# V loads moved to ScalarE's DMA queue, and two more groups of x transposed by DMA

## The chip, the cores and the metric

The kernel runs on one core of a Trainium2 chip. The metric is device time in microseconds (us): a kernel is run several times beside runs of the kernel before on the same chip, and the median is given. All profiles show one execution. The engines are TensorE (PE; its weight loads are PEld), VectorE (DVE), ScalarE (ACT), GpSimd (POOL) and SyncE (SP). DMAs are issued by SyncE, ScalarE or GpSimd; the queue of an issuing engine is written with a q (SPq, ACTq, POOLq).

## The reference, cut to what matters

```python
q, k, v : (8, 8, 576, 64) fp32        # batch, heads, sequence, head_dim
# attention inside chunks of 64 positions
scores = scale * matmul(q_c, k_c.T);  attn = softmax(scores);  out = matmul(attn, v_c)
x = out.transpose(0, 2, 1, 3).reshape(4608, 512)
# FFN with squared ReLU: w_in (512, 2048), w_out (2048, 512)
h = maximum(x @ w_in, 0);  return (h * h) @ w_out
```

## The kernel before

The 4608 tokens are cut into 18 groups of 256. Two groups make a block, which is the unit of the FFN; block 0 holds groups 0 and 1, block 1 groups 3 and 2, block 2 groups 4 and 5, and so on to block 8. While TensorE computes the FFN of block j, the attention of block j+1 is slipped in at fixed "slots" between the FFN's matmul groups, and q, k and v of block j+2 ("far") are loaded.

Each group passes through these steps. The short names are those of the plan of slots.

- Loads of q, k (L110) and v (L117 and L124), from SyncE.
- C: GpSimd casts q and k to bf16 (L217). TD: a DMA transpose turns them (L224, from SyncE).
- SC: scores (L238) on TensorE. AV: values (L259), then the division on VectorE (L269), which gives x.
- XT: x is transposed, either by TensorE with a VectorE copy (L292, L296) or by a DMA from SyncE (L282).

```python
    def transpose_x(g):                                    # XT
        ...
        if g >= FIRST_DMA_X:                               # 6
            for t in range(2):
                x = state.pop(("x", g, t))
                nc.sync.dma_start_transpose(
                    out=xTs[j][:, :, c + t * 128:c + (t + 1) * 128],
                    in_=x.rearrange("p h a d -> p (h a d)"))
            return
        ...                                                # 8 TensorE transposes, 1 VectorE copy
```

ScalarE computes the Relu between the two FFN products, copies the second product out of PSUM and issues the store. All of this is one stream of instructions, in order:

```python
    # ffn_in: first product (L319), Relu (L325), square on VectorE (L326)
            nc.scalar.activation(out=rl[:, 0:n], in_=h[:, 0:n], func=AF.Relu)
    # ffn_out: second product (L335), one token tile of 128 after the other
                    nc.scalar.copy(out=o_sb, in_=o_ps)                      # L352
                    nc.scalar.dma_start(out=out[t0:t0 + 128, :], in_=o_sb)  # L353
```

The block loop takes one load at each slot in `go_slots`, then runs the attention steps planned for that slot. In the built program the DMAs of SyncE and ScalarE draw their completion semaphores from one set of eight, in rotation, and each DMA waits until the one eight places before it has landed, whichever queue issued that one.

The softmax here doesn't subtract the row's maximum and nothing guards it: scores larger than these inputs give would overflow.

Of the kernel before, what the change touches and what calls it, by code (L numbers as in the profile page):

```python
# [17 lines left out]
def kernel(  # L18
# [9 lines left out]
    nc = tc.nc  # L28
# [11 lines left out]

    blocks = [[0, 1], [3, 2]] + [[g, g + 1] for g in range(4, n_grp, 2)]
    FIRST_DMA_T = 4
    FIRST_DMA_X = 6
    BT = GT * max(len(b) for b in blocks)

    const_pool = ctx.enter_context(tc.tile_pool(name="const", bufs=1))
# [28 lines left out]
    def segments(g0, n):  # L75
        while n:
            b, s = divmod(g0, S)
            m = min(n, S - s)
            yield b, s, m
            g0 += m  # L80
            n -= m
# [3 lines left out]
    def runs(g):  # L85

        for t in range(GT // 128):
            p = 0
            for b, s, m in segments(g * GT + t * 128, 128):
                yield t, p, m, b, s  # L90
                p += m

    def qk_pieces(g):
        q_sb = in_pool.tile([128, 2, H, D], FP32, name="q_sb")
        k_sb = in_pool.tile([128, 2, H, D], FP32, name="k_sb")
        qk[g] = (q_sb, k_sb)
        if g < FIRST_DMA_T:

            p = 0
            for b, s, m in segments(g * GT, GT):  # L100
                for dst, src in ((q_sb, q), (k_sb, k)):
                    yield lambda dst=dst, src=src, b=b, s=s, p=p, m=m: nc.sync.dma_start(
                        out=dst.rearrange("p t h d -> p (t h d)")[p:p + m // 2, :].rearrange(
                            "p (h e) -> p h e", h=H),
                        in_=src[b, :, s:s + m, :].rearrange("h (s i) d -> s h (i d)", i=2))
                p += m // 2
            return
        for t, p, m, b, s in runs(g):
            for dst, src in ((q_sb, q), (k_sb, k)):
                yield lambda dst=dst, src=src, b=b, s=s, t=t, p=p, m=m: nc.sync.dma_start(  # L110
                    out=dst[p:p + m, t, :, :],
                    in_=src[b, :, s:s + m, :].rearrange("h s d -> s h d"))

    def v_pieces(g):

        for t, p, m, b, s in runs(g):
            yield lambda t=t, p=p, m=m, b=b, s=s: nc.sync.dma_start(  # L117
                out=v_even[g % NV][p:p + m, t, :, 0:D],
                in_=v[b, 0::2, s:s + m, :].rearrange("h s d -> s h d"))
        for n in {0: [0, 1, 2], 2: [5], 3: [6, 7, 8]}.get(g, [2 * g + 1, 2 * g + 2]):  # L120
            lo, hi = max(0, 128 * n - 64), min(n_tokens, 128 * n + 64)
            p = lo - (128 * n - 64)
            for b, s, m in segments(lo, hi - lo):
                yield lambda n=n, p=p, m=m, b=b, s=s: nc.sync.dma_start(  # L124
                    out=v_odd[n % NO][p:p + m, :, 0:D],
                    in_=v[b, 1::2, s:s + m, :].rearrange("h s d -> s h d"))
                p += m

    def go(pieces):
        for f in pieces:  # L130
            f()
# [143 lines left out]
    def transpose_x(g):  # L275
        j, c = place[g]
        if j not in xTs:
            xTs[j] = att_pool.tile([128, n_dt, BT], BF16, name="xT", bufs=2)
        if g >= FIRST_DMA_X:
            for t in range(2):  # L280
# [20 lines left out]
    SC, AV, XT = scores, values, transpose_x  # L301
# [10 lines left out]
    def ffn_in(j, c, n):  # L312
        if j not in gTs:
            gTs[j] = ffn_pool.tile([128, n_ft, BT], BF16, name="gT")
        gT, xT = gTs[j], xTs[j]
        for ft in range(n_ft):
            h = ps_ffn.tile([128, 512], FP32, name="ps_ffn")
            for dt in range(n_dt):
                nc.tensor.matmul(  # L319
                    out=h[:, 0:n],  # L320
                    lhsT=w_in_bf[:, dt, ft * 128:(ft + 1) * 128],
                    rhs=xT[:, dt, c:c + n],
                    start=(dt == 0), stop=(dt == n_dt - 1))
            rl = ffn_pool.tile([128, 512], BF16, name="rl", bufs=3)
            nc.scalar.activation(out=rl[:, 0:n], in_=h[:, 0:n], func=AF.Relu)  # L325
            nc.vector.tensor_tensor(  # L326
                out=gT[:, ft, c:c + n], in0=rl[:, 0:n], in1=rl[:, 0:n], op=ALU.mult)
            yield

    def ffn_out(j):  # L330
        gT = gTs.pop(j)
        for tt in range(len(blocks[j]) * GT // 128):
            o_ps = ps_ffn.tile([128, d_model], FP32, name="ps_ffn")
            for ft in range(n_ft):
                nc.tensor.matmul(  # L335
                    out=o_ps,
                    lhsT=gT[:, ft, tt * 128:(tt + 1) * 128],
                    rhs=w_out_bf[:, ft, :],
                    start=(ft == 0), stop=(ft == n_ft - 1))
                if ft == n_ft - 1:  # L340
                    t0 = blocks[j][tt // 2] * GT + tt % 2 * 128
                    if j == len(blocks) - 1 and tt == 2 * len(blocks[j]) - 1:
                        for copy, dma, c in ((nc.scalar.copy, nc.scalar, 0),
                                             (nc.vector.tensor_copy, nc.sync, 256)):
                            o_sb = ffn_pool.tile([128, d_model], FP32, name="o_sb", bufs=4)
                            copy(out=o_sb[:, 0:256], in_=o_ps[:, c:c + 256])
                            dma.dma_start(
                                out=out[t0:t0 + 128, c:c + 256], in_=o_sb[:, 0:256])
                        yield
                        continue  # L350
                    o_sb = ffn_pool.tile([128, d_model], FP32, name="o_sb", bufs=4)
                    nc.scalar.copy(out=o_sb, in_=o_ps)  # L352
                    nc.scalar.dma_start(out=out[t0:t0 + 128, :], in_=o_sb)  # L353
                if ft % 4 == 3:
                    yield
# [27 lines left out]
    def pieces(grps):  # L383
        for g in grps:
            yield from qk_pieces(g)
        for g in grps:
            yield from v_pieces(g)
# [27 lines left out]
    for j, grps in enumerate(blocks):  # L415
        nxt = blocks[j + 1] if j + 1 < len(blocks) else []
        far = blocks[j + 2] if j + 2 < len(blocks) else []
        plan = {}

        def at(slot, f, g):  # L420
            plan.setdefault(slot, []).append((f, g))

        if j == 0:
            loads, go_slots = iter(()), []
            for slot, f in ((24, T), (27, SC), (29, AV), (31, XT)):
                at(slot, f, nxt[0])
            at(31, T, nxt[1])
            phases = [ffn_in(0, 0, 512), ffn_out_by_ft(0)]
        elif j == 1:
            go_slots = [*range(17), *range(34, 48)]  # L430
            loads = itertools.chain(pieces(nxt), pieces(far))
            for slot, f in ((2, SC), (6, AV), (11, XT)):
                at(slot, f, grps[1])
            for i, g in enumerate(nxt):
                for slot, f in ((22 + 4 * i, C), (27 + 4 * i, TD), (36, SC), (38 + 2 * i, AV),
                                (42 + 2 * i, XT)):
                    at(slot, f, g)
            phases = [ffn_in(1, 0, 256), ffn_in(1, 256, 256), ffn_out(1)]
        else:
            loads, go_slots = pieces(far), range(32)  # L440
            d = {2: 5, 3: 2}.get(j, 0)
            if j == 2:
                go_slots = [*range(10), *range(18, 32)]
            for i, g in enumerate(nxt):
                for slot, f in ((4, SC), (8, AV), (11, XT)):
                    at(slot + d if f is SC else slot + d + 3 * i, f, g)
            for i, g in enumerate(far):
                at(14 + 2 * i, C, g)
                at(19 + 3 * i, TD, g)
            phases = [ffn_in(j, 0, len(grps) * GT), ffn_out(j)]  # L450
        slot = 0
        for phase in phases:
            for _ in phase:
                if slot in go_slots:
                    for f in loads:
                        f()
                        break
                for f, g in plan.get(slot, []):
                    f(g)
                slot += 1  # L460
        go(loads)
        if j == 1:
            for g in far:
                C(g)
                TD(g)
# [30 lines left out]
```

## Time and profile before

| | before |
|---|---|
| median of the first runs | 303.29 us (300.78 to 303.96, 3 runs) |
| span of the profiled run | 302.7 us |
| TensorE busy | 280.5 us, 93% |
| blocks 2 to 7, start to start | 31.07, 30.50, 30.15, 31.22, 29.36, 29.36 us |
| idle before block 2's first FFN product | none |

Last, from the table by stretch (stretch, its length, busy us and count of each engine, granted clock, DMA share, GB/s), blocks 3 and 5, as the yardstick for later:

```profile
120.65:151.15 30.50, 29.34 (x253) 13.62 (x257) 10.10 (x24) 13.76 (x22) 4.50 (x4) 1.00 1.04 206
...
181.30:212.52 31.22, 29.44 (x254) 13.57 (x257) 11.69 (x24) 12.98 (x22) 4.58 (x4) 1.00 0.93 199
```

TensorE is busy for all but 1.2 us of block 3 and all but 1.8 us of block 5, at full clock.

### The profile page before, as it was taken

The numbers are of one execution on the slowest core, as the hardware profiler recorded it, in microseconds if no ns is written. First come the engines' busy times: TensorE is split into PE (matmuls) and PEld (weight loads), VectorE is DVE, ScalarE is ACT, GpSimd is POOL, SyncE is SP. The second block draws the span as 40 slices with busy tenths as digits, with TensorE's granted clock in tenths as the row PEclk, the third lists the DMA queues.
The fourth block names the chain that finished last, engine by engine and source line by source line (L and its number), as shares of the span: only waits on it lengthen the run. The fifth ranks groups of instructions, "written<-read, shape, count | busy, mean of one in ns | idle before, by whom it ended". The sixth has DMA issues, their size and how long they took to land.

```text
span 302.7 us, 6379 instructions
## 1 busy us (share of the span) xinstructions
PE 280.5 (93%) x2564; PEld 141.3 (47%) x2598; DVE 113.0 (37%) x247; ACT 130.0 (43%) x225; POOL 49.4 (16%) x68
## 2 busy tenths in 40 slices
PE   2889979898899799899999997999999999999995
PEld 2654435784454444444444443444444444444442
DVE  1348613692234350353037203740482038104400
ACT  1536305674217621762176215731662186217511
POOL 2047820140130040023003201400230000000000
PEclk9999999999799999999999999999999999999999
DMA  7999999999999899999899899869997704211011
GB/s 207 243 347 365 342 264 246 237 206 212 217 213 211 194 191 205 224 215 193 195 250 211 148 229 269 171 104 254 267 183 157 182 37 37 69 69 38 0 69 69
DMA packets 158765, 57.04 MB, mean 188 GB/s; under 512 B 139664, under 2 KB 152208, under 8 KB 158736
## 3 DMA queue, kind: packets, MB, share of 16 engines
q1 hardware_dynamic: 153024, 46.81, 73.2%
q10 hardware_dynamic: 5712, 9.83, 10.4%
q8 instruction: 20, 0.33, 0.5%
q14 instruction: 9, 0.07, 0.1%
HBM read 36.70 MB, written 9.44 MB: 152 GB/s over the span
## 4 chain that ended last, share of the span: by engine, by line
PE 67%; DMA 18%; SPq 10%; issue 2%; POOL 1%; ACT 1%; DVE 0%; ACTq 0%
PE ps_ffn L319 31%; PE ps_ffn L335 27%; DMA qkT<-qkb 6%; DMA k_sb<-in_k_dram 6%; SPq L224 4%; DMA w_st<-in_moe_w_in_dram 4%; SPq L282 3%; PE ps_att L259 2%; PE ps_ffn L364 2%; DMA w_st<-in_moe_w_out_dram 2%; PE ps_att L238 2%; SPq L117 1%; PE ps_ffn L164 1%; SPq L124 1%; POOL w_in_bf L139 1%
## 5 line engine op out<-in xcount | busy, mean ns | idle before, releaser
L319 PE MATMUL ps_ffn<-xT,w_in_bf 128*128 128x512 bf16 (+1 forms) x620 | 128.6, 357 | 3.1 <-ACT rl L325 1.6
L326 DVE TENSOR_TENSOR gT<-rl 128x512 bf16<-128x512 bf16 (+1 forms) x160 | 75.5, 489 | 133.9 <-ACT rl L325 131.4
L335 PE MATMUL ps_ffn<-w_out_bf,gT 128*128 128x512 bf16 x500 | 113.0, 382 | 0.8 <-issue 0.3
L325 ACT ACTIVATE rl<-ps_ffn 128x512 bf16<-128x512 f32 (+1 forms) x160 | 86.2, 560 | 42.5 <-PE ps_ffn L319 31.0
L319 PEld LDWEIGHTS <-w_in_bf 128*128 128x128 bf16 x640 | 60.8, 98 | 60.9 <-issue 2.1
L335 PEld LDWEIGHTS <-gT 128*128 128x128 bf16 x512 | 49.9, 98 | 59.7 <-issue 1.3
L352 ACT COPY o_sb<-ps_ffn 128x512 f32<-128x512 f32 x31 | 18.2, 586 | 92.9 <-PE ps_ffn L335 79.7
L217 POOL CAST qkb<-q_sb 128x1024 bf16<-128x1024 f32 x14 | 14.7, 1048 | 146.9 <-DMA q_sb<-in_q_dram 126.6
L269 DVE TENSOR_TENSOR x<-ps_att,rec 128x512 bf16<-128x512 f32 x36 | 24.9, 691 | 1.2
L245 ACT ACTIVATE e<-ps_att 128x1024 bf16<-128x1024 f32 x18 | 18.2, 1037 | 5.5 <-PE ps_att L238 5.5
L217 POOL CAST qkb<-k_sb 128x1024 bf16<-128x1024 f32 x14 | 16.0, 1144 | 6.5 <-DMA k_sb<-in_k_dram 6.4
L364 PE MATMUL ps_ffn<-w_out_bf,gT 128*128 128x512 bf16 x62 | 14.4, 379 | 0.2 <-issue 0.2
L238 PE MATMUL ps_att<-qkT 64*64 64x64 bf16 x576 | 8.1, 198 | 6.0 <-DMA qkT<-qkb 4.6
L266 DVE RECIPROCAL rec<-ps_att 128x8 f32<-128x8 f32 x36 | 7.1, 199 | 15.4 <-PE ps_att L259 15.4
L139 POOL CAST w_in_bf<-w_st 128x1024 bf16<-128x1024 f32 (+1 forms) x9 | 8.8, 980 | 19.1 <-DMA w_st<-in_moe_w_in_dram 19.1
L238 PEld LDWEIGHTS <-qkT 64*64 64x64 bf16 x576 | 6.2, 110 | 10.8 <-DMA qkT<-qkb 6.1
L259 PEld LDWEIGHTS <-e 64*64 64x64 bf16 x576 | 6.8, 110 | 8.5 <-DVE x L269 3.0
L259 PE MATMUL ps_att<-vo_sb,e 64*64 64x65 bf16 x288 | 9.2, 199 | 0.8 <-DMA vo_sb<-in_v_dram 0.8
L364 PEld LDWEIGHTS <-gT 128*128 128x128 bf16 x64 | 6.0, 98 | 7.2 <-issue 0.3
L147 POOL CAST w_out_bf<-w_st 128x1024 bf16<-128x1024 f32 x8 | 8.7, 1091 | 2.7 <-DMA w_st<-in_moe_w_out_dram 2.6
L259 PE MATMUL ps_att<-ve_sb,e 64*64 64x65 bf16 x288 | 9.2, 199 | 0.0
L173 ACT COPY qkT<-ps_att 128x512 bf16<-128x512 bf16 x4 | 2.1, 589 | 13.9 <-DVE qkT L173 11.8
(31 smaller groups left out, 46.0 us busy)
## 6 DMA issues: line engine op xcount, KB each, us to landing
out_dram<-o_sb ACTq DMA_DIRECT2D x35, 256.0 KB, 3.3
q_sb<-in_q_dram SPq DMA_DIRECT2D x25, 256.0 KB, 4.8
k_sb<-in_k_dram SPq DMA_DIRECT2D x25, 256.0 KB, 5.3
ve_sb<-in_v_dram SPq DMA_DIRECT2D x32, 128.0 KB, 3.9
vo_sb<-in_v_dram SPq DMA_DIRECT2D x32, 128.0 KB, 3.9
w_st<-in_moe_w_out_dram SPq DMA_DIRECT2D x8, 512.0 KB, 5.7
w_st<-in_moe_w_in_dram SPq DMA_DIRECT2D x7, 512.0 KB, 7.3
q_sb<-in_q_dram SPq DMA_DIRECT2D x3, 512.0 KB, 6.6
```

The costliest lines, as they stand in the source:

```text
L217: nc.gpsimd.tensor_copy(out=qkb[:, which], in_=qk[g][which].rearrange("p t h d -> p (t h d)"))
L224: nc.sync.dma_start_transpose(out=qkT.rearrange("c w t h q -> c (w t h) q"), in_=qkb.rearrange("p w c -> p (w c)"))
L238: nc.tensor.matmul(out=ps[64 * c:64 * c + 64, o0:o0 + 64], lhsT=qkT[64 * a:64 * a + 64, 1, t, hp, cols], rhs=qkT[64 * a:64 * a + 64, 0, t, ...
L245: nc.scalar.activation(out=e.rearrange("p a h t q -> p (a h t q)"), in_=ps, func=AF.Exp, scale=scale)
L259: nc.tensor.matmul(out=ps[64 * p:64 * p + 64, a, hp * (D + 1):(hp + 1) * (D + 1)], lhsT=e[64 * c:64 * c + 64, a, hp, t, :], rhs=vb[64 * c: ...
L269: nc.vector.tensor_tensor(out=x.rearrange("p h a d -> p a h d"), in0=o[:, :, :, 0:D], in1=rec.to_broadcast([128, 2, n_hp, D]), op=ALU.mult)
L319: nc.tensor.matmul(out=h[:, 0:n], lhsT=w_in_bf[:, dt, ft * 128:(ft + 1) * 128], rhs=xT[:, dt, c:c + n], start=(dt == 0), stop=(dt == n_dt ...
L325: nc.scalar.activation(out=rl[:, 0:n], in_=h[:, 0:n], func=AF.Relu)
L326: nc.vector.tensor_tensor(out=gT[:, ft, c:c + n], in0=rl[:, 0:n], in1=rl[:, 0:n], op=ALU.mult)
L335: nc.tensor.matmul(out=o_ps, lhsT=gT[:, ft, tt * 128:(tt + 1) * 128], rhs=w_out_bf[:, ft, :], start=(ft == 0), stop=(ft == n_ft - 1))
L352: nc.scalar.copy(out=o_sb, in_=o_ps)
L364: nc.tensor.matmul(out=o_ps[tt], lhsT=gT[:, ft, tt * 128:(tt + 1) * 128], rhs=w_out_bf[:, ft, :], start=(ft == 0), stop=(ft == n_ft - 1))
```

## The change

It is meant to relieve two engines. V loads leave SyncE's queue, so that the q/k transposes there are issued earlier. Groups 4 and 5 have their x transposed by DMA as the later groups have, which frees TensorE of 16 transposes. (The change was described as touching groups 2 to 5; the limit that the code moves touches 4 and 5 alone.) The far block's V loads are issued by ScalarE during the second product, one at each slot in `v_slots`.

```diff
-    FIRST_DMA_X = 6
+    FIRST_DMA_X = 4
 ...
-    def v_pieces(g):
+    def v_pieces(g, eng=nc.sync):
 ...   # both V loads: nc.sync.dma_start -> eng.dma_start
         elif j == 1:
-            go_slots = [*range(17), *range(34, 48)]
-            loads = itertools.chain(pieces(nxt), pieces(far))
+            go_slots, v_slots = [*range(17), *range(34, 48)], range(34, 48)
+            loads = itertools.chain(pieces(nxt), *map(qk_pieces, far))
 ...
-                                (42 + 2 * i, XT)):
+                                (41 + 2 * i, XT)):
 ...
         else:
-            loads, go_slots = pieces(far), range(32)
-            d = {2: 5, 3: 2}.get(j, 0)
-            if j == 2:
-                go_slots = [*range(10), *range(18, 32)]
+            go_slots, v_slots = range(16), range(17, 32)
+            loads = itertools.chain(*map(qk_pieces, far))
+            d = {2: 5, 3: 2}.get(j, 1)
 ...
+        v_loads = itertools.chain(*(v_pieces(g, nc.scalar) for g in far if j))
 ...   # at each slot, one of `loads` and one of `v_loads`
         go(loads)
+        go(v_loads)
```

More of the change, by code (lines that the diff above doesn't have):

```diff
@@ L112, in qk_pieces @@
                     in_=src[b, :, s:s + m, :].rearrange("h s d -> s h d"))
-    def v_pieces(g):
+    def v_pieces(g, eng=nc.sync):
         for t, p, m, b, s in runs(g):
-            yield lambda t=t, p=p, m=m, b=b, s=s: nc.sync.dma_start(
+            yield lambda t=t, p=p, m=m, b=b, s=s: eng.dma_start(
                 out=v_even[g % NV][p:p + m, t, :, 0:D],
@@ L123, in v_pieces @@
             for b, s, m in segments(lo, hi - lo):
-                yield lambda n=n, p=p, m=m, b=b, s=s: nc.sync.dma_start(
+                yield lambda n=n, p=p, m=m, b=b, s=s: eng.dma_start(
                     out=v_odd[n % NO][p:p + m, :, 0:D],
@@ L423 @@
         if j == 0:
-            loads, go_slots = iter(()), []
+            loads, go_slots, v_slots = iter(()), [], []
             for slot, f in ((24, T), (27, SC), (29, AV), (31, XT)):
@@ L453 @@
             for _ in phase:
-                if slot in go_slots:
-                    for f in loads:
-                        f()
-                        break
+                for queue, slots in ((loads, go_slots), (v_loads, v_slots)):
+                    if slot in slots:
+                        for f in queue:
+                            f()
+                            break
                 for f, g in plan.get(slot, []):
```

## The prediction

> **What bounds the kernel now.** I began with the page of the kernel before, its busy table and its slices.
>
> ```profile
> PE 280.5 (93%) x2564; PEld 141.3 (47%) x2598; DVE 113.0 (37%) x247; ACT 130.0 (43%) x225; POOL 49.4 (16%) x68
> ...
> PE   2889979898899799899999997999999999999995
> ...
> PEclk9999999999799999999999999999999999999999
> DMA  7999999999999899999899899869997704211011
> ```
>
> TensorE is busy for 93% of the span, and the DMA engines are nearly full until slice 31 of 40. So only TensorE's gaps can be won, together with the one slice in which its clock was at 0.7. Next I read TensorE's timeline, where the gaps stand in brackets.
>
> ```profile
> 76.25 0.45 PE L238 MATMUL ps_att<-qkT 64*64 64x64 bf16 x32 [1.67 <-DMA qkT<-qkb]
> 76.86 2.88 PE L335 MATMUL ps_ffn<-w_out_bf,gT 128*128 128x512 bf16 x7 [0.16 <-issue]
> ...
> 84.36 0.61 PE L292 MATMUL ps_att<-ident,x 128*128 128x128 bf16 x8
> 84.81 1.89 PE L335 MATMUL ps_ffn<-w_out_bf,gT 128*128 128x512 bf16 x8
> 86.54 0.61 PE L292 MATMUL ps_att<-ident,x 128*128 128x128 bf16 x8
> ...
> 100.27 0.45 PE L238 MATMUL ps_att<-qkT 64*64 64x64 bf16 x32 [1.39 <-DMA qkT<-qkb]
> ...
> 128.18 0.45 PE L238 MATMUL ps_att<-qkT 64*64 64x64 bf16 x32 [0.95 <-DMA qkT<-qkb]
> ```
>
> The scores of the second group of a block wait for a DMA transpose of q and k. Blocks 2 to 8 start their first FFN product at 89.58, 120.65, 151.15, 181.30, 212.52, 241.88 and 271.24 us, so blocks 2 to 5 take 31.07, 30.50, 30.15 and 31.22 us. Blocks 6 and 7 take 29.36 each and have no such gap. Against 29.36, blocks 2 to 5 lose 1.71 + 1.14 + 0.79 + 1.86 = 5.5 us in all. That is the most that relief of the queues can give there. Block 5's loss is of another kind: ScalarE's Relu was held for 2.00 us by a k load, because an output store ahead of it in ScalarE's queue waited for that load.
>
> Then I read SyncE's queue, to see why the q/k transposes come late.
>
> ```profile
> 107.74 1.45 SPq L117 DMA_DIRECT2D ve_sb<-in_v_dram  x2
> 109.31 3.92 SPq L282 DMA_TRANSPOSE xT<-x  x2
> 113.29 1.25 SPq L124 DMA_DIRECT2D vo_sb<-in_v_dram  x2
> 114.64 2.57 SPq L282 DMA_TRANSPOSE xT<-x  x2
> 117.31 2.89 SPq L224 DMA_TRANSPOSE qkT<-qkb  x1
> 120.25 0.60 SPq L124 DMA_DIRECT2D vo_sb<-in_v_dram  x1
> 120.95 1.10 SPq L117 DMA_DIRECT2D ve_sb<-in_v_dram  x2
> 122.15 3.62 SPq L224 DMA_TRANSPOSE qkT<-qkb  x1
> ```
>
> V loads stand between the transposes, and the queue is occupied without a break. The transpose begun at 122.15 lands 5.99 us later by the chain, just ahead of the matmul at 128.18.
>
> **What the Trainium skill says.** "DMA: Bandwidth & Descriptors", section "Issuing engines are not separate DMA queues": DMAs of all issuing engines share the same 16 DMA engines, so a second issuer saves only the sequencer's issue time. The trace agrees as far as it goes: a V load takes about 0.6 us of SyncE's queue, and the DMA row is at 8 to 9 tenths however little data moves. "TensorE: Matmul & The Clock Gate", section "Why this matters for your kernels": idle gaps of more than about 3 us drop the clock to half. Here a smaller gap was enough: after the 1.67 us gap seven matmuls took 2.88 us, 0.41 each, against 1.89 us for eight, 0.24 each, at 84.81. The same page, "Architectural detail", calls ScalarE's queue strict FIFO. The held Relu in block 5 agrees, and it matters for every load put on that queue.
>
> **The change, part by part.**
> (1) Transposes of x. The words say groups 2 to 5, but the limit moves from 6 to 4 and the built program loses exactly 16 transpose matmuls (groups 4 and 5) and two VectorE copies. TensorE gets 2 x 0.45 us back by the chain's steps at 84.53 and 86.70, so -0.9 us. The copies (2 x 0.69) were beside other work. Four DMA transposes of 1.2 us issue each, 3.1 us from issue to landing, come on SyncE.
> (2) V loads of the blocks two ahead leave SyncE's queue: 9 to 10 a block, about 0.6 us each, 5 to 6 us. So q/k transposes come earlier, and the waits at 100.27 (1.39), 128.18 (0.95), 156.60 (0.60) and block 5's hold should go, unless something replaces them.
> (3) Eight completion semaphores serve all DMAs of both queues in turn: in the built program each DMA waits for the one eight places before it, on whichever queue. SyncE therefore waits for V loads that ScalarE issues, and the reverse. This decides the seam from block 1 to block 2, where the new x transposes have least time.
>
> The seam, on the clock of the kernel before; the two are alike up to the q/k transposes at 69.10. The second output copy of block 1 runs at 81.47 to 82.06. Behind it ScalarE issues a store (0.4) and then a V load at 82.5. The first x transpose waits for that load by its semaphore; V lands 3.9 us after issue by the page (I take 3.5, as it is alone on its ring), so 86.0. x itself is ready at 81.1, and is not what holds it. After that SyncE's order is fixed: two x transposes (2 x 1.2), a q and a k load (2 x 0.65), two x transposes. The fourth starts at 86.0 + 2.4 + 1.3 + 1.2 = 91.0 (rounded up) and lands 3.1 later, at 94.1. TensorE would be ready for block 2 at 89.58 - 0.9 = 88.7, and its first matmul reads all 512 columns. That is a new stall of 5.4 us, with 4 to 7 within the spread of the landings. The clock should drop after it: the slow stretch after 76.25 cost 7 x 0.19 us plus some 0.5 on what followed, about 1.9 us; I take 1.7.
>
> Block 2 then reaches its scores about 14 us after the last x transpose's issue; q/k transposes for groups 6 and 7 have landed by about 100.5 by the same counting, so the 1.39 goes. At the seam to block 3, the V loads on ScalarE wait for the q/k transposes and a q load on SyncE, and hold the last two output copies: by the same steps the copy of the third token tile ends 16.4 us after block 2's second product starts, when the third FFN group of block 3 wants its bank at 16.0, and the first Relu follows at 17.8. A stall of about 0.6 us takes most of the place of the 0.95. From block 4 on SyncE has some 15 us of issue (8 loads at 0.65, 4 x 1.2, 2 x 2.4) in 29.4, and I find no new wait.
>
> Sum in us: -0.9 (matmuls) +5.4 (stall) +1.7 (clock) -1.4 (block 2) -0.3 (block 3) -0.8 (block 4) -1.9 (block 5) = +1.8. On the median of 303.29 this is 305.1; I shade it to 304.8, because V alone on its ring may land sooner than I took.
>
> **Rivals.** First, the pure gain: x transposes land in time, and the change gives 0.9 + 5.5 = 6.4 us at best, 296.9. For it: SyncE is relieved, and the order of slots has visibly been tuned (x one slot earlier). Against it: after x of group 5 is ready at 84.4 there are under 5 us to the seam, and four x transposes with two loads need 6.1 us of issue plus a landing, even from 84.4. A milder form, a stall of 2 us without clock loss, gives 303.29 - 0.9 + 2 - 4.4 = 300.0. Second, nothing gained on DMA: the 16 engines are the limit (DMA row at 9 tenths), so q/k land no sooner although issued earlier, and waits of 1.39, 0.95 and 0.60 stay beside the new stall: 303.29 - 0.9 + 5.4 + 1.7 = 309.5. Against it: the DMA row falls to 1 to 4 tenths in 0.75 us slices near 103 and 112 us, just where SyncE sits on a wait, so the engines have room. Third, ScalarE becomes the hold: V loads that wait for SyncE's DMAs delay copies and Relu in every block, 1 us for each of six blocks, 311. Against it: the third and fourth copy have some 3 us until their banks are wanted, and V is all issued by mid-product in the later blocks.
>
> **Range and chances.** The stall (4 to 7) and the clock (0 to 2.5) give about 2.5 us each way; block 3's and 4's seams add 1.5, and the runs of before themselves span 3.2. Hence 300.3 to 309.0. Faster by 2% needs 297.2, nearly the whole pure gain: 0.06. Slower by 2% needs 309.4, the second rival or the third: 0.09. The rest is 0.85.
>
> **What would show it.** TensorE's gap before the first FFN product of block 2, released by the x transpose, should be 4 to 7 us, with a PEclk digit below 9 in that slice. SyncE's first x transpose should stand waiting for a V load near 86. The waits of 1.39, 0.95 and 0.60 and the Relu's 2.00 should be absent, and blocks 4 and 5 should be at 29.4 to 29.6. I am wrong if that gap is under 2 us (V lands in 2 us, or the wait is not the one eight back), if blocks 3 to 5 keep waits on q/k, or if Relu or the output copies wait for DMAs in most blocks.

## More of the kernel before

The prediction shows the busy table, the slices, TensorE's timeline and SyncE's queue; they are not repeated. Four other views matter later. First the DMA issues of the kernel before, with count, size, and the median us from issue to landing:

```profile
vo_sb<-in_v_dram SPq DMA_DIRECT2D x32, 128.0 KB, 3.9
...
qkT<-qkb SPq DMA_TRANSPOSE x14, 4.9
```

Next TensorE's entry into block 2. The columns are start, us, engine, line, operation, tiles and count; a bracket at the end would show idle time and its cause. There is none, so block 2 follows block 1 at once:

```profile
89.58 8.80 PE L319 MATMUL ps_ffn<-xT,w_in_bf 128*128 128x512 bf16 x39
```

Third, from the list of waits (us in total, times, longest), the one wait of TensorE on SyncE's DMAs that recurs through the kernel:

```profile
PE ps_att L238 <- DMA qkT<-qkb: 4.6, 4, 1.7
```

## The result and the profile after

| | before | after |
|---|---|---|
| median | 302.12 us (300.78 to 303.96, 4 runs) | 322.79 us (321.31 to 324.49, 4 runs) |
| ratio of fast runs, 95% interval | | 1.0682 (1.0587 to 1.0777) |
| span of the profiled run | 302.7 us | 322.7 us |
| blocks 2 to 7, start to start | 31.07, 30.50, 30.15, 31.22, 29.36, 29.36 | 31.63, 33.78, 32.27, 35.62, 31.89, 29.37 |
| start of block 2 | 89.58 us | 96.82 us |

Ratios here and below are the mean time of one kernel's fast runs over the mean of the other's fast runs of the same rounds, so they are not quite the ratio of the quoted medians. The change is 20 us slower, well outside the predicted range of 300.3 to 309.0.

The page of the kernel after, TensorE, its clock and the DMA engines in 40 slices of 8.1 us:

```profile
PE   2789998998809999599989996999979999999995
...
PEclk9989999999957999999999998799999999999999
DMA  8999999999999779975996699569994960420011
```

The slice at 0 is new, and so are most of the dips that follow it: 5 (from 129 us), 8 (from 161), 6 (from 194) and 7 (from 234). They stand at or just after the seams at 128.45, 162.23, 194.50 and 230.12 us. The clock stands at 5 in the empty slice and at 7 in the next, and at 8 and 7 after 194 us. The DMA row has dips of its own, to 5 and 6, from the middle on.

Adding up where the 20.0 us between the spans lie: block 2 starts 7.24 later; block 2 itself takes 0.56 more, block 3 3.28, block 4 2.12, block 5 4.40, block 6 2.53, block 7 0.01; block 8 and the tail 0.14 less. So there are two losses: 7.2 us before block 2, and 12.3 us in blocks 3 to 6.

**The first loss, before block 2.** TensorE's timeline after, at the line that answers to the 89.58 of before:

```profile
96.82 10.61 PE L319 MATMUL ps_ffn<-xT,w_in_bf 128*128 128x512 bf16 x39 [9.25 <-DMA xT<-x]
```

TensorE was idle for 9.25 us for the DMA transposes of x, and the same 39 matmuls then took 10.61 us in place of 8.80, because the clock had dropped. SyncE's queue shows why x came late:

```profile
86.74 3.56 SPq L282 DMA_TRANSPOSE xT<-x  x2
90.35 0.58 SPq L110 DMA_DIRECT2D q_sb<-in_q_dram  x1
90.99 0.68 SPq L110 DMA_DIRECT2D k_sb<-in_k_dram  x1
91.77 3.24 SPq L282 DMA_TRANSPOSE xT<-x  x2
```

This is the order that the prediction gave, and the first transpose starts at 86.74 for its 86.0. It waited for the V load with which it shares a semaphore (shown below): ScalarE issued that load at 81.30, and it took 5.4 us to land. But the pairs took 3.56 and 3.24 us to issue, not 2.4 each: one by one, 2.26 and 1.21, then 1.93 and 1.21. The last one began at 93.80 and landed at 96.73.

**The second loss, at every later seam.** In the list of waits after, these four stand out. Before, only the second was there, with 1.6 us, once:

```profile
PE ps_ffn L319 <- ACT o_sb L352: 6.0, 4, 2.2
...
PE ps_ffn L319 <- ACT rl L325: 4.1, 3, 1.8
...
ACT o_sb L352 <- DMA ve_sb<-in_v_dram: 23.6, 4, 9.4
...
ACT o_sb L352 <- DMA q_sb<-in_q_dram: 8.8, 1, 8.8
```

TensorE waits for ScalarE to empty a bank (o_sb) or to finish a Relu (rl), and ScalarE sat idle for up to 9.4 us before a copy until a DMA let it go on. Not all of such a wait is loss: before, ScalarE sat idle for 2.87 us between two of these copies, while TensorE made the next token tile. ScalarE's timeline at the seam from block 2 to block 3 shows one such hold from the inside:

```profile
123.22 0.37 ACTq L353 DMA_DIRECT2D out_dram<-o_sb  x1
130.25 0.38 ACTq L117 DMA_DIRECT2D ve_sb<-in_v_dram  x1
...
131.96 0.58 ACT L352 COPY o_sb<-ps_ffn 128x512 f32<-128x512 f32 x1 [8.76 <-DMA q_sb<-in_q_dram]
```

Between 123.6 and 130.25 ScalarE did nothing. It stood at a V load that could not be issued yet, and the output copy behind that load stood with it until 131.96. The copy's data had been ready for about 7 us by then: the second product ends at 128.4, and before, the copies of these tiles follow each other by 3.45 us, so the third tile was done near 125. The chain of waits says what the load was waiting for (start, us, what):

```profile
123.00 7.23 DMA qkT<-qkb
...
130.25 4.23 DMA ve_sb<-in_v_dram
...
134.56 0.36 ACTq L353
...
135.67 2.76 PE ps_ffn L319 x12
```

The q/k transpose of group 9 lands at 130.23, and ScalarE issues its V load 0.02 us later. That V load takes 4.23 us to land, and only then may the output store at 134.56 be issued, and the Relu behind it, and TensorE's matmuls at 135.67. The V load reads nothing that the transpose wrote. The built program gives the link: both use the same completion semaphore. The entries in question, each with the DMA that it waits for by its semaphore (HW0 to HW7):

```
x transpose, group 4, first   SyncE    HW7  <-  V load         ScalarE
q/k transpose, group 9        SyncE    HW0  <-  x transpose    SyncE
V load (ve)                   ScalarE  HW0  <-  q/k transpose, group 9   SyncE
V load (vo)                   ScalarE  HW3  <-  q load         SyncE
output store                  ScalarE  HW0  <-  V load (ve)    ScalarE
```

The table by stretch gives the same blocks 3 and 5 as above:

```profile
128.45:162.23 33.78, 29.83 (x253) 13.64 (x257) 11.54 (x24) 12.57 (x22) 4.35 (x4) 1.00 0.98 181
...
194.50:230.12 35.62, 32.20 (x253) 14.21 (x256) 9.98 (x24) 13.27 (x22) 4.29 (x4) 0.90 0.96 171
```

Length less PE busy is TensorE's idle time: 3.95 us in block 3, where it was 1.16, and 3.42 in block 5, where it was 1.78. In block 5 the matmuls themselves also took 2.8 us longer, at a granted clock of 0.90. Summed over blocks 3 to 6, idle time grew by 8.0 us and busy time by 4.3. The bytes moved per us fell (206 to 181 GB/s in block 3), so more data in the same time was not what delayed the DMAs.

Landings did get longer, in the median. The two lines of the DMA issues that answer to those of before:

```profile
vo_sb<-in_v_dram ACTq DMA_DIRECT2D x21, 128.0 KB, 5.5
...
qkT<-qkb SPq DMA_TRANSPOSE x14, 5.4
```

A V load of odd heads takes 5.5 us from ScalarE's queue where it took 3.9 from SyncE's, and the q/k transposes 5.4 in place of 4.9. V of even heads stays at 3.9.

### The profile page after: what moved, and what is told of

It reads as the page before. It is cut to its first block, busy times and chain, and to the rows that moved or that the text cites. A ratio compares the mean times of both kernels' runs of the same rounds, so it can differ in the third digit from the quotient of the medians.

```text
span 322.7 us, 6341 instructions
## 1 busy us (share of the span) xinstructions
PE 285.5 (88%) x2548; PEld 142.3 (44%) x2582; DVE 111.0 (34%) x245; ACT 128.3 (40%) x225; POOL 48.7 (15%) x68
## 4 chain that ended last, share of the span: by engine, by line
PE 53%; DMA 17%; SPq 12%; DVE 7%; issue 5%; ACT 5%; ACTq 1%
PE ps_ffn L319 28%; PE ps_ffn L335 16%; DMA k_sb<-in_k_dram 6%; SPq L224 6%; PE ps_ffn L364 4%; DMA qkT<-qkb 4%; DVE gT L326 4%; DMA vo_sb<-in_v_dram 3%; ACT rl L325 3%; SPq L282 3%; DMA ve_sb<-in_v_dram 3%; DVE x L269 2%; PE ps_att L259 1%; SPq L102 1%; PE ps_att L238 1%
## 5 line engine op out<-in xcount | busy, mean ns | idle before, releaser
L319 PE MATMUL ps_ffn<-xT,w_in_bf 128*128 128x512 bf16 (+1 forms) x620 | 134.9, 366 | 21.1 <-DMA xT<-x 9.2
L326 DVE TENSOR_TENSOR gT<-rl 128x512 bf16<-128x512 bf16 (+1 forms) x160 | 74.7, 485 | 159.4 <-ACT rl L325 156.0
L335 PE MATMUL ps_ffn<-w_out_bf,gT 128*128 128x512 bf16 x500 | 111.4, 379 | 0.8 <-issue 0.3
L325 ACT ACTIVATE rl<-ps_ffn 128x512 bf16<-128x512 f32 (+1 forms) x160 | 84.8, 560 | 54.6 <-PE ps_ffn L319 40.5
L319 PEld LDWEIGHTS <-w_in_bf 128*128 128x128 bf16 x640 | 61.5, 99 | 84.2 <-issue 19.3
L217 POOL CAST qkb<-k_sb 128x1024 bf16<-128x1024 f32 x14 | 15.3, 1089 | 7.2 <-DMA k_sb<-in_k_dram 4.1
L364 PE MATMUL ps_ffn<-w_out_bf,gT 128*128 128x512 bf16 x62 | 14.4, 380 | 0.2 <-issue 0.2
```

The source lines that it names most:

```text
L217: nc.gpsimd.tensor_copy(out=qkb[:, which], in_=qk[g][which].rearrange("p t h d -> p (t h d)"))
L319: nc.tensor.matmul(out=h[:, 0:n], lhsT=w_in_bf[:, dt, ft * 128:(ft + 1) * 128], rhs=xT[:, dt, c:c + n], start=(dt == 0), stop=(dt == n_dt ...
L326: nc.vector.tensor_tensor(out=gT[:, ft, c:c + n], in0=rl[:, 0:n], in1=rl[:, 0:n], op=ALU.mult)
L335: nc.tensor.matmul(out=o_ps, lhsT=gT[:, ft, tt * 128:(tt + 1) * 128], rhs=w_out_bf[:, ft, :], start=(ft == 0), stop=(ft == n_ft - 1))
L364: nc.tensor.matmul(out=o_ps[tt], lhsT=gT[:, ft, tt * 128:(tt + 1) * 128], rhs=w_out_bf[:, ft, :], start=(ft == 0), stop=(ft == n_ft - 1))
```

## The experiments

Three theories were to be told apart.

- **Place in SyncE's queue** for the first loss: x is transposed late because its DMAs stand behind other DMAs. The rival: the DMA engines have no room there.
- **ScalarE held by shared semaphores** for the second: any load in ScalarE's instruction stream that waits for SyncE's DMAs holds copies and Relus. The first rival: V arrives late or the engines are short of room, whoever issues. The second: the later blocks suffer only because of what happened before block 2.
- The two losses add up, or one hides part of the other, or makes it larger.

Eleven kernels ran. All gave correct results. The median of the kernel before was 300.69 us in the first call (7 runs), 302.51 in the second (11) and 301.22 in the third (11).

### x_only: the x transposes alone (kernel before with one number changed)

```diff
-    FIRST_DMA_X = 6
+    FIRST_DMA_X = 4
```

> The kernel before with x of groups 4 and 5 transposed by DMA as the only edit (V stays on SyncE's queue, slots as before). Theory 'two separate losses' (a seam stall from the x transposes, and ScalarE held at shared DMA semaphores by its V loads): only the first is here. TensorE stands 2 to 5 us before block 2 waiting for xT and loses up to 2 us of clock, blocks 3 to 6 stay at 29.3 to 31.3 us each; 304 to 309 us in all. Rival 'the extra DMA transposes cost everything, as transposes crowd the DMA engines': 315 us or more. Rival 'V on ScalarE is the whole loss': 302 us or less.

Measured: 304.55 us (303.49 to 307.11), ratio 1.0141 (1.0062 to 1.0221). TensorE's entry into block 2:

```profile
92.26 11.22 PE L319 MATMUL ps_ffn<-xT,w_in_bf 128*128 128x512 bf16 x39 [5.33 <-DMA xT<-x]
```

So there is a gap even with no V load on ScalarE, and the slow clock after it (11.22 us for 8.80). Blocks 3 and 4 then run at 29.37 us each, where they took 30.50 and 30.15 before. The x transposes by themselves cost the seam and nothing later. The gap is just above the 2 to 5 us expected.

### v_only: the V loads alone (kernel after, one number back)

```diff
-    FIRST_DMA_X = 4
+    FIRST_DMA_X = 6
```

> The changed kernel with x of groups 4 and 5 still transposed on TensorE; V loads on ScalarE's queue. Theory 'two separate losses': no stall before block 2 (gap under 1 us), but the output copies of blocks 2 to 5 are still held 5 to 9 us at V loads, and blocks 3 to 6 still take 32 to 35 us; 311 to 316 us. Rival 'the seam sets off all that follows': blocks 3 to 6 fall back to about 29.5 us and the time to about 300 us.

Measured: median 314.99 us over four runs. Two of them (316.31 and 316.50) count as slow, since they are over 1.5% above the fastest (310.36). The ratio uses the other two: 1.0377 (1.0256 to 1.0498). There is no stall before block 2 (it starts at 88.53), and ScalarE's hold is there; from its list of waits:

```profile
ACT o_sb L352 <- DMA qkT<-qkb: 12.4, 2, 9.1
```

The profiled run is the fastest of the four, at a span of 308.6, and shows blocks 3 to 6 at 32.04, 31.21, 33.08 and 31.86 us, in all 7.0 over before. So the V loads alone bring the second loss and not the first, though two of the four blocks came out below the 32 to 35 us expected. The runs scatter by 6 us, so its size is known only roughly here.

### v_slots_sync: the kernel after with the V loads back on SyncE, at the same slots

```diff
-        v_loads = itertools.chain(*(v_pieces(g, nc.scalar) for g in far if j))
+        v_loads = itertools.chain(*(v_pieces(g, nc.sync) for g in far if j))
```

> The changed kernel with the V loads at the same slots, but issued by SyncE. Theory 'ScalarE held by V loads': the holds of output copies vanish (no copy held over 3 us by a V load), blocks 3 to 6 take 29.4 to 31.5 us, the seam stall stays at 3 to 9 us; 304 to 311 us. Rival 'it is where the V loads stand in the order, whichever queue': blocks 3 to 6 stay at 32 to 35 us and the time at 318 us or more.

Measured: 308.99 us (308.08 to 309.94), ratio 1.0267 (1.0193 to 1.0340).

```profile
97.39 11.32 PE L319 MATMUL ps_ffn<-xT,w_in_bf 128*128 128x512 bf16 x39 [10.64 <-DMA xT<-x]
```

The first loss is all there. The V loads now stand in SyncE's queue as well, and block 2 starts 0.57 us later than after the whole change. The second loss is gone: blocks 3 to 6 take 29.37, 29.90, 29.39 and 29.51 us. One word removes it, at the same slots. Do the two losses add? 2.7% here for the seam and 3.8% in v_only for the holds make 6.5%, beside 6.8% for the whole change. But both runs also hold the new slots and order of loads, which cost 0.9% alone (sync_x6 below). Counted from there, the seam adds 1.75 points and the holds 2.85, and 1.3 points of the whole change, some 4 us, are left. With intervals of half a point to 1.2 points each way, that the losses simply add is not shown. x_only's 1.4% is smaller, since there nearly all V loads follow the x transposes in SyncE's queue: the first x transpose starts at 82.63 us there, and here, behind V loads issued between the q and k loads from 74 us on, at 88.33.

### v_gpsimd: the same with GpSimd as issuer

```diff
-        v_loads = itertools.chain(*(v_pieces(g, nc.scalar) for g in far if j))
+        v_loads = itertools.chain(*(v_pieces(g, nc.gpsimd) for g in far if j))
```

> The changed kernel with the V loads at the same slots, issued by GpSimd, which has completion semaphores of its own, so that no V load waits for a DMA of SyncE or the reverse. Theory 'shared semaphores couple the two queues': blocks 3 to 6 at 29.4 to 31 us, seam stall 3 to 7 us, 303 to 309 us. Rival 'the 16 DMA engines are the limit, a second stream beside q and k slows them': q and k still land in over 5.3 us and blocks 3 to 6 stay at 32 us or more, 317 us or more. GpSimd's own casts may come later behind its V loads; if so, waits on the q/k transposes return at the scores and the run says nothing on the rival.

Measured: 319.02 us (313.30 to 326.24), ratio of the two fast runs 1.0474 (1.0353 to 1.0595); the profiled run was slow. TensorE waited 3.66 and 6.66 us for q/k transposes in block 1, and block 3 took 37.4 us. Late casts, which the expectation allowed for, are not the reason there: GpSimd had done the casts by 66.5 us. From 66.4 to 73.0 us it then issued nine V loads in a row, and the two transposes that SyncE began at 68.19 and 71.74 took 10.5 and 14.1 us to land, where they took 5.0 and 4.0 before. That speaks for the rival, a second stream that slows the transposes. Since this profile is of a slow run, the rival is taken up again at td_first_gps, whose runs are all fast.

### sync_x6: only the slots and the order of loads that the change brings (V on SyncE, x transposes as before)

```diff
-    FIRST_DMA_X = 4
+    FIRST_DMA_X = 6
-        v_loads = itertools.chain(*(v_pieces(g, nc.scalar) for g in far if j))
+        v_loads = itertools.chain(*(v_pieces(g, nc.sync) for g in far if j))
```

> Both parts of the change taken back where the first runs put the losses: V at the changed kernel's slots but issued by SyncE, and x of groups 4 and 5 transposed on TensorE again; the slot shifts stay. Theory 'two separate losses, additive': no stall before block 2 (gap under 1 us), blocks 3 to 6 at 29.4 to 30.0 us as in the run with V on SyncE; about 4 us better than the kernel before in blocks 3 to 5, less what the wait of 1.4 us in block 2 keeps: 297 to 300 us, ratio 0.985 to 0.995. Rival 'blocks 3 to 6 ran clean there only because TensorE came 10 us later out of the seam': without the seam stall, waits on the q/k transposes of 0.5 to 1.5 us a block return in blocks 3 to 5, and the time is that of the kernel before, ratio 0.995 to 1.005.

Measured: 304.16 us (303.52 to 306.13), ratio 1.0092 (1.0042 to 1.0142). Blocks 3 to 7 are clean at 29.4 to 29.8 us, as expected, but the 297 to 300 us expected in all was missed, by one new wait in block 2:

```profile
100.97 0.45 PE L238 MATMUL ps_att<-qkT 64*64 64x64 bf16 x32 [3.75 <-DMA qkT<-qkb]
```

In block 1 the V loads now go out between the q and k loads of groups 6 and 7, so the last q and k arrive later, and so do their casts and transposes. This is a cost of the new order in block 1 alone. After the gap the matmuls also ran slowly, and block 2 took 35.0 us for the 31.07 of before.

### sync_x6_sc: the same, with the scores of a block's second group two slots later

```diff
-(36, SC)                                     # block 1
+(36 + 2 * i, SC)
-at(slot + d if f is SC else slot + d + 3 * i, f, g)
+at(slot + d + (2 * i if f is SC else 3 * i), f, g)
```

> As the run before it, and the scores of the second group of a block moved two slots later (about 1.7 us), in block 1 and in all later blocks. Theory: the waits for the second group's q/k transpose (1.0 to 1.7 us in block 1, 1.4 in block 2) and the slow clock that can follow the first are gone; 1.5 to 4 us less than the run before it. Rival 'the wait only moves to the values': a wait of the same size stands before the values instead and the time is within 0.5 us of it.

Measured: 301.25 us (300.10 to 304.26), ratio 0.9989 (0.9936 to 1.0041): the wait in block 2 fell to 1.48 us, and the kernel is level with before. Giving the consumer two slots more takes most of a wait away without touching a DMA.

### td_first: the same, and in block 1 the far q/k transposes go ahead of the far V loads

```diff
-            go_slots, v_slots = [*range(17), *range(34, 48)], range(34, 48)
+            go_slots, v_slots = [*range(17), *range(34, 48)], ()
 ...
         go(loads)
-        go(v_loads)
         if j == 1:
             for g in far:
                 C(g)
                 TD(g)
+        go(v_loads)
```

> As the run before it, and at the seam of block 1 the q/k casts and transposes for groups 6 and 7 go to SyncE's queue ahead of the nine V loads of those groups. Theory: they land about 5 us sooner, no wait on them in block 2, and V still lands in time: 0 to 1 us less. Rival: V of group 6 now comes late and the values of block 2 wait 1 us or more for it: 0 to 2 us more.

Measured: 299.94 us (298.35 to 301.02), ratio 0.9928 (0.9883 to 0.9972). Block 2 starts at 87.95, earlier than before, and blocks 2 to 7 take 29.58 to 29.71 us. TensorE's list of waits no longer has q/k transposes.

This answers the rival that the later blocks ran clean in v_slots_sync and x_only only because a late block 2 gave the DMAs time. Here nothing is late, and they are clean. (The scores stand two slots later here; in tuned below those of block 4 on are back at v_slots_sync's slots, and blocks 4 to 7 take 29.4 us each.) It also answers the rival of room: with the same V bytes in the same blocks, block 3 takes 29.59 us at 209 GB/s.

### seam_x_first: are the x transposes late for want of room, or for their place?

This is the kernel before with the x transposes of groups 4 and 5 on DMA, and with all far loads of block 1 put behind them.

```diff
-    FIRST_DMA_X = 6
+    FIRST_DMA_X = 4
-            go_slots = [*range(17), *range(34, 48)]
+            go_slots = range(17)
```

> The kernel before with x of groups 4 and 5 by DMA and all loads for groups 6 and 7 moved behind the x transposes of block 1 in SyncE's queue. Theory 'the seam stall is the place of the x transposes in SyncE's queue (loads, and the semaphores of loads, ahead of them)': the gap before block 2 falls from 5.3 us to 0.5 to 3 us; in return block 2's scores wait 3 to 7 us for q/k. Rival 'four x transposes cannot land faster with the DMA engines as full as they are': gap stays at 5 us or more.

Measured: 310.91 us (309.27 to 312.64), ratio 1.0300 (1.0239 to 1.0361). Block 2 starts at 85.53 us with no gap at all. So x arrives in time when nothing stands ahead of it, and TensorE is relieved as intended. But the far loads now come later, and the scores pay:

```profile
103.84 0.65 PE L238 MATMUL ps_att<-qkT 64*64 64x64 bf16 x32 [9.52 <-DMA qkT<-qkb]
```

The gap moved from the seam to block 2's scores and grew, from x_only's 5.33 us to 9.52, more than the 3 to 7 expected. So place in the queue is the cause of the first loss. But in this part of the kernel the queue is full: of the two orders tried, each made TensorE wait for the DMAs that came second.

### td_first_act: the clean kernel with one word changed

```diff
-(v_pieces(g, nc.sync) for g in far if j)
+(v_pieces(g, nc.scalar) for g in far if j)
```

> The run with the q/k transposes first, with one word changed: the V loads of the blocks two ahead are issued by ScalarE. No x transpose by DMA stands at the seam here, so only the hold of ScalarE can show. Theory 'ScalarE is held at the shared semaphores': blocks 3 to 6 go from 29.6 to 31 to 34 us each, output copies wait 4 to 9 us behind V loads, and each long wait of ScalarE ends when the DMA eight places back lands; 6 to 13 us more, 305 to 313 us. Rival 'V on ScalarE costs only where the seam is late': within 2 us of the run it is made from.

Measured: 322.36 us (321.27 to 323.23), ratio 1.0745 (1.0695 to 1.0794) over the kernel before. Against td_first, 299.94 us on another chip, that is some 22 us (by the two ratios to the kernel before 8.2%, or 25 us), more than the 6 to 13 expected. The blocks agree: 2 to 6 take 8.0, 3.6, 2.4, 4.4 and 3.6 us more than td_first's, 22.0 in all. From its waits:

```profile
ACT o_sb L352 <- DMA qkT<-qkb: 21.5, 3, 9.5
...
ACT rl L325 <- DMA vo_sb<-in_v_dram: 10.2, 2, 8.3
```

The V loads of block 1 now stand ahead of the first Relus of block 2 in ScalarE's stream, and leave ScalarE idle for 8.3 us before one; TensorE idles for 6.1 us for that Relu (at 98.57). That accounts for most of block 2's 8.0. The added x transposes are not in this kernel, so the whole cost is that of moving V to ScalarE: the hold, and what the second queue adds to the landings. The q/k transposes land in 6.3 us in the median, in td_first in 5.0.

### td_first_gps: V loads away from both queues

```diff
-(v_pieces(g, nc.sync) for g in far if j)
+(v_pieces(g, nc.gpsimd) for g in far if j)
```

> The same kernel with the V loads issued by GpSimd, behind its casts this time, with completion semaphores of its own and a queue of its own. Theory 'waits at shared semaphores, not the room in the DMA engines': no V load is held by q, k or transposes; blocks 3 to 6 at 29.6 to 30.5 us, 298 to 303 us. A part may remain, as output stores now stand eight places behind the transposes more often: then ScalarE's waits name the transposes and blocks take up to 31.5 us. Rival 'a second stream beside q and k slows every load, and that is the loss': q and k land in 5.3 us or more, blocks 3 to 6 at 31 to 34 us, 306 us or more.

Measured: 316.88 us (316.40 to 318.46), ratio 1.0573 (1.0511 to 1.0635). This was meant as the cure and was not one. Blocks 4 and 5 are clean (29.63 and 30.08 us), but block 3 takes 41.07 and block 6 35.97. The chain at block 3:

```profile
122.60 7.24 DMA q_sb<-in_q_dram
...
129.92 0.34 ACTq L353
...
131.00 5.28 PE ps_ffn L319 x12
```

No V load is on ScalarE or in its set of semaphores. Now it is ScalarE's output store (L353) that waits until a q load of SyncE has landed, at 129.84, and the Relu behind the store waits with it. In the built program these two share a semaphore. With the V loads gone from the rotation, output stores come eight places behind q/k transposes and q loads that are still in flight. So ScalarE can be held without a V load in its stream, by any DMA there that shares a semaphore with a late DMA of SyncE.

Why SyncE's DMAs were late is the rival's answer. From 113.34 us on GpSimd issued nine V loads in 6.4 us. Of the two q/k transposes issued beside them, the trace says:

```profile
DMA to landing us min/median/max: 8.6/9.8/11.0
```

In td_first the same two landed in 4.1 and 4.9 us. The rival's 306 us or more came true too, so this run does not decide against it. It shows the two at work together: a second stream makes the landings late, and the shared semaphore carries the delay to ScalarE. The coupling is in the kernel before as well, where a k load held one Relu of block 5 for 2.00 us through an output store.

### tuned: td_first with the scores placed by need

The second group's scores come one slot later in block 1, two in block 2, and as in the kernel after from then on, since the later blocks have no such wait left.

```diff
-(36 + 2 * i, SC)
+(36 + i, SC)
-at(slot + d + (2 * i if f is SC else 3 * i), f, g)
+at(slot + d + ((2 * i if j == 2 else 0) if f is SC else 3 * i), f, g)
```

> Candidate for the best: the run with the q/k transposes first, with the scores of the second group only one slot later in block 1, two in block 2, and side by side again in the later blocks. Theory: each later block loses the two gaps of about 0.1 us that splitting the scores made, 29.6 to 29.4 us a block, and the wait of 1.0 us on the reciprocal in block 1 goes; 1 to 2.5 us less than that run, 297.5 to 299 us, ratio 0.982 to 0.990. Rival: in block 1 the wait on the q/k transpose comes back with its slow clock, 0 to 2 us more.

Measured: 297.85 us (296.80 to 298.65), beside 301.22 (298.17 to 302.83) of before; ratio 0.9932 (0.9880 to 0.9984), span 295.3. It beats both kernels, though by under 1%. The 1 to 2.5 us that the slots were to gain over td_first did not show: td_first's ratio is 0.9928. The wait that began the case is nearly gone; in this kernel's list of waits:

```profile
PE ps_att L238 <- DMA qkT<-qkb: 0.2, 1, 0.2
```

Neither the V loads on ScalarE nor the added x transposes are in it. What it keeps of the change is that V has slots of its own, behind q and k in the later blocks, and the shifted slots. It adds, in block 1, the q/k transposes ahead of V, and the slots of the scores.

## Why the prediction was wrong

**The losing step** follows the reckoning of the seams: "From block 4 on SyncE has some 15 us of issue (8 loads at 0.65, 4 x 1.2, 2 x 2.4) in 29.4, and I find no new wait", with block 3's stall put at 0.6 us. That step predicted a gain of 0.3 + 0.8 + 1.9 = 3.0 us in blocks 3 to 5. Those three blocks lost 9.8 us, and block 6 another 2.5. The step counted SyncE's issue time, which was indeed not the limit: with V on SyncE as well, blocks 3 to 6 of v_slots_sync took 29.37 to 29.90 us. It did not follow the rotation into ScalarE's stream in those blocks, as it had done at the seams before. Shown by: the hold in the trace with its 0.02 us from landing to issue, the loss vanishing with one word (v_slots_sync), and the loss coming back, at 22 us, with one word in a kernel without the x transposes (td_first_act).

**The third rival was the true one.** "ScalarE becomes the hold" was listed, with 1 us for each of six blocks. What was set against it, "the third and fourth copy have some 3 us until their banks are wanted", failed by size: at the seam to block 3 a copy was held for about 7 us. Nor was V all issued by mid-product: at the seam to block 4 three V loads went out after 163 us, when block 4 had begun at 162.23.

**Block 3** shows the same in small. The prediction saw the mechanism there (V loads that wait for q/k transposes and hold the last two copies) and sized the stall at 0.6 us. It measured 2.25 us for the copy and 1.04 for the Relu. The reason is instructive. The prediction reckoned with 2.4 us of issue for a q/k transpose; what it took for the landing it does not say, and the page's median is 4.9. But at this very place the trace of before had 2.89 and 3.62 us of issue (they stand in the prediction's own fence of SyncE's queue) and 5.99 to land for the second. After the change it was 6.95 for the pair and 7.23 to land. So of the time that ScalarE waited, most was to be read beforehand; only some 1.2 us of landing and 0.4 of issue came with the change. The median over the kernel hid the crowded place. At the next two seams the longer landing weighs more: the transpose that held ScalarE took 7.9 and 8.1 us to land, where the same ones took 4.7 and 4.5 before.

**The seam to block 2: right mechanism, too small.** Predicted 5.4 us (4 to 7), measured 9.25. The first x transpose was foreseen to 0.7 us. The term that was off is the issue of the first transpose of each pair: 2.26 and 1.93 us for the 1.2 taken, 1.8 in all. The 1.2 fits the median of the four x transposes near 109 to 116 us before (1.23), but one of these took 2.61, and the prediction's own fence shows the two pairs at 3.92 and 2.57 us. With the first transpose's 0.7, 0.4 of small gaps in the queue, and 0.2 off for a quicker landing, x arrived 2.7 us late (96.8 for 94.1). TensorE was also ready 1.1 us earlier (87.57, against 88.7), since after its gap near 76 us, now 0.98 us, no matmul ran slowly. Together that is the 3.85 us missing. The clock's loss was 1.8 us for 1.7 predicted.

**The shading** downwards, "V alone on its ring may land sooner than I took", was wrong in its direction: from ScalarE's queue V took 5.5 us (odd heads) and 3.9 (even heads) in the median, and the load that held the first x transpose 5.4, not under 3.5. That this transpose was still foreseen to 0.7 us was luck in part: the load went out at 81.30, not 82.5, and landed 1.9 us more slowly than taken.

**What was right:** block 2's wait of 1.39 us went, and block 7 stayed at 29.37. The first rival, the pure gain, did not occur. Of the second, that q/k would land no sooner, one half is true: after the change TensorE waits only once for a q/k transpose (1.0 us in all, against 4.6), but each takes longer to land.

**What stays open.** No run changed the semaphores alone; that they are the link is read from the built program and from the times of landing and issue, and the runs agree with it. Nor did a run separate the hold from the longer landings: moving V off SyncE's queue, by whichever engine, brought both. At the seam to block 3 the longer landing is about 1.2 us of a hold of 7; at the seams to blocks 4 and 5 it is over 3 us each, about half of the hold or more (an estimate from the idle times of 9.40 and 8.47 us before those copies, less the usual 2.87). Why the first x transpose of a pair takes up to 2.3 us to issue and the second 1.2 was not tried.

## What to carry to other kernels

Before a load is moved to an engine that also computes, list for each such load what its issue waits for, including the semaphore that it shares with DMAs of other queues. If that can be late, every instruction behind it can be late by as much. Look also at which DMAs the moved loads will now run beside, since these can land later. In this kernel load issue was best left with SyncE, which does nothing else, and the gain sought in the order of its DMAs and in when their consumers run. Size a DMA's issue and landing by the same place in the trace of before, not by the page's median, and look for the tightest seam rather than the mean room of the queue.

## What the Trainium skill lacked or had wrong

- "DMA: Bandwidth & Descriptors", section "Issuing engines are not separate DMA queues", says that a second issuer saves only the sequencer's time. It does not say that it can cost far more: with loads on ScalarE it sat idle for up to 9.4 us before an output copy, and one word in td_first cost some 22 us of 300.
- No page that I found has it that DMAs of two queues may share completion semaphores in rotation, so that one queue waits for the other without a dependence of data. Here a transpose landed at 130.23 us and a V load of the other queue was issued at 130.25; in td_first_gps a q load landed at 129.84 and an output store of the other queue was issued at 129.92.
- The same page, section "Queues, rings and completion order", says that each DMA engine goes round-robin between the queues that have work, packet by packet. That fits the longer landings with a second busy queue, but it gives no size for them. In td_first the q/k transposes landed in 5.0 us in the median, with V on ScalarE or GpSimd in 6.3; two of them beside nine V loads of GpSimd took 8.6 and 11.0.
- "TensorE: Matmul & The Clock Gate", section "Why this matters for your kernels", puts the gap that drops the clock at about 3 us. Here the length of the gap alone did not decide it below 3 us. In the kernel before, seven matmuls took 2.88 us after a gap of 1.67 us, and in the kernel after eight took 2.75 after one of 1.93. But after gaps of 2.25 (kernel after) and 2.46 us (td_first_act) eight took 2.04, where eight at full clock take 1.89. After gaps of 5.3 to 10.6 us, 39 matmuls took 10.6 to 11.3 us in place of 8.80.
- No page that I found says that the issue of DMA transposes of the same size differs from one to the next: for x, 1.21 us and 2.26 us side by side at the seam of the kernel after, and 1.20 to 2.61 us among four in the kernel before.
